# Attention with grouped keys: two early loads held back until the first has landed, and one set of transposes moved behind the third score chunk

## The chip, the cores and the metric

The kernel runs on one core of one Trainium2 chip. The metric is the device time of one execution in microseconds (us). PE is the matmul engine, ACT the engine that takes exponentials, DVE and POOL the two other vector engines, SP the engine whose queue issues most loads. A trace is one profiled execution; its span runs from the first to the last instruction and is about 1.7 us shorter than the device time. A load is issued by a queue and, some us later, lands: then all its data are there and the engines that wait for it may go on. PE starts at half clock and its granted clock then rises to full: in the trace of before the record of the clock has the rise at 4.57 us, the six weight loads of fillers from 3.8 to 4.3 us take 151 ns each, and those after 5.9 us 98 ns.

## The reference, cut to what matters

```python
B, Hq, Hkv, Sq, Sk, D = 16, 32, 8, 288, 512, 128      # bf16, four query heads per key head
scores = einsum("bhqd,bhkd->bhqk", q, k) * D ** -0.5
p = softmax(scores, axis=-1)
out = einsum("bhqk,bhkd->bhqd", p, v)
```

There are 16 x 8 = 128 groups. A group is the 4 x 288 = 1152 query rows that share one K and one V of 512 rows. The kernel cuts a group into three chunks, so there are 384 chunks.

## The kernel before

For chunk n PE computes the transposed scores S(n) = K Q^T (1536 columns of PSUM), ACT takes exp of all of them in one instruction, and two chunks later (`LAG`) PE multiplies by V: PV(n-2). DVE scales and stores. A column of ones beside V gives the row sums.

K and Q must have D on the partitions. Most come by transposed loads from SP. K of groups 0 and 1 take another way, to be there sooner: ACT's queue loads them plainly and PE transposes them. Q of group 0 comes in three transposed loads, one for each chunk.

```python
def op_kd(eng, g):                       # plain load of K of group g (0 or 1)
    eng.dma_start(kd_sb[:, g], kd_v[:, g]).then_inc(sem["s_kd%d" % g], 16)
def op_kt(g, tiles, bank): ...           # PE: four 128x128 transposes into ps_o
def op_kc(g, tiles, bank, n): ...        # DVE: copies them into kt_sb (s_k<g>)
def op_q0(i):                            # one third of Q of group 0
    c0, c1 = i * TPC, (i + 1) * TPC
    nc.sync.dma_start_transpose(qt_sb[:, 0, c0:c1], q_v[0:P, c0 * D:c1 * D]).then_inc(sem["s_qp%d" % i], 16)
def op_warm(n, w, dst): ...              # n filler matmuls on zeros, w columns each
# ... cut ...
first = [lambda i=i: op_q0(i) for i in range(NC)]           # SP: Q of group 0 in thirds,
first += [lambda: op_q(1), lambda: op_k(0, 2), lambda: op_q(2), lambda: op_v(0, None, 2, UG), lambda: op_q(3)]

@block.tensor
def _(eng):
    op_warm(WARM, BANK, ps_o[:, 1])
    op_kt(0, range(NJ), 0)
    op_warm(6, P, ps_s[:, 1])
    for n in range(NS):
        if n == LAG:
            op_kt(1, range(NJ), 1)
            op_warm(4, P, ps_o[:, 0])
        op_s(n)                          # waits: K, Q, and ACT's chunk n-2 (two PSUM halves)
        if n >= LAG:
            op_pv(n - LAG)

@block.scalar
def _(eng):
    op_kd(eng, 0)
    emit(eng, [("s_one", 1)], lambda: eng.activation(dum[:, 1:2], dum[:, 0:1], ACTF.Exp))
    op_v(0, eng, 0, 2)                   # V of groups 0 and 1
    op_kd(eng, 1)
    for n in range(NS):
        op_exp(n)
# ... cut: POOL copies V beside the ones, DVE scales, checks of the sums ...
```

Of the kernel before, what the change touches and what calls it, by code (L numbers as in the profile page):

```python
# [123 lines left out]
def bass_standalone__gqa_softmax__near_ridge_kernel(  # L124
# [5 lines left out]
):  # L130
    B, Hq, Sq, D = q.shape
    _, Hkv, Sk, _ = k.shape
    P = 128
    R = (Hq // Hkv) * Sq
    NJ = Sk // P
# [13 lines left out]
    LAG = 2  # L149
# [20 lines left out]
    with ExitStack() as es:  # L170
# [31 lines left out]
        def choose(eng, key):  # L202
            eng.wait_ge(sem["s_flag"], 1)
            reg = eng.alloc_register("bad_" + key)
            eng.load(reg, flag_i[:])
            if key == "sp":
                for (s, n) in need(eng, stored()):
                    eng.wait_ge(s, n)
            eng.br_ne(reg, 0, "general_" + key, "done_" + key)
            with nc.body("general_" + key):  # L210
                if key == "sp":
                    eng.sem_inc(sem["s_go"], 1)
                fns[key](eng)
                eng.br("done_" + key)
            nc.switch_bb("done_" + key)
# [18 lines left out]
        ps_s = main.enter_context(nc.psum_tensor("ps_s", [P, 2, CH], FP32))  # L234
# [4 lines left out]
        def need(eng, waits):  # L239

            left = []
            for (s, n) in waits:
                key = (id(eng), s)
                if seen.get(key, 0) < n:
                    seen[key] = n
                    left.append((sem[s], n))
            return left

        def emit(eng, waits, fn):
            waits = need(eng, waits)  # L250
            for (s, n) in waits[:-1]:
                eng.wait_ge(s, n)
            ins = fn()
            if waits:
                ins.wait_op(waits[-1][0], waits[-1][1], "sem-ge")
            return ins
# [3 lines left out]
        def op_kd(eng, g):  # L260
            eng.dma_start(kd_sb[:, g], kd_v[:, g]).then_inc(sem["s_kd%d" % g], 16)
# [12 lines left out]
        def op_v(u, eng=None, g0=0, g1=UG):  # L274
            eng = eng or nc.sync
            sl = u % NSLOT
            if u >= NSLOT:
                for (s, n) in need(eng, [("s_vc", UG * (u - NSLOT + 1))]):
                    eng.wait_ge(s, n)
            eng.dma_start(  # L280
                vd_sb[:, sl, g0:g1], v_v[:, u * UG + g0:u * UG + g1]
            ).then_inc(sem["us_v%d" % sl if u > 0 else "s_v%d" % g0], 16)
# [13 lines left out]
        def have_q(g, i):  # L296
            if g == 0:
                return ("s_qp%d" % i, 16)
            return ("s_q%d" % (g % NQ), 16 * (g // NQ + (0 if g % NQ == 0 else 1)))

        def have(kind, g):

            u = g // UG
            if u == 0 and kind == "k":
                return ("s_k%d" % min(g, 2), (1, 1, 16)[min(g, 2)])
            if u == 0:
                return ("s_v%d" % (g // 2 * 2), 16)
            return ("us_%s%d" % (kind, u % NSLOT), 16 * (u // NSLOT + (0 if u % NSLOT == 0 else 1)))
# [22 lines left out]
        def op_kt(g, tiles, bank):  # L331

            eng = nc.tensor
            dst = ps_o[:, bank].bitcast(BF16)
            for x, j in enumerate(tiles):
                ins = emit(eng, [("s_id", 2), ("s_kd%d" % g, 16)], lambda: eng.transpose(  # L336
                    dst[:, x * P:(x + 1) * P], kd_sb[:, g, j * D:(j + 1) * D], ident[:]))
            ins.then_inc(sem["s_kp"], 1)
# [7 lines left out]
        def op_warm(n, w, dst):  # L346

            for x in range(n):
                emit(nc.tensor, [("s_z", 1)], lambda: nc.tensor.matmul(  # L349
                    dst[:, 0:w], z_sb[:, 0:P], z_sb[:, 0:w], start=True, stop=True))  # L350

        def op_s(n):
            eng = nc.tensor
            g, i = n // NC, n % NC
            sl, gi = (g // UG) % NSLOT, g % UG
            waits = [have("k", g), have_q(g, i)]
            if n >= 2:
                waits.append(("s_e", n - 1))
            qg = qt_sb[:, g % NQ, i * TPC:(i + 1) * TPC].rearrange("d t p -> d (t p)")
            for x, (c, j, r0, w) in enumerate(pieces):  # L360
                ins = emit(eng, waits if x == 0 else [], lambda: eng.matmul(  # L361
                    ps_s[:, n % 2, c:c + w], kt_sb[:, sl, j, gi, :], qg[:, r0:r0 + w], start=True, stop=True))
                if n == 0 and c + w == BANK:
                    ins.then_inc(sem["s_s0"], 1)
            ins.then_inc(sem["s_s"], 1)
# [7 lines left out]
        def op_pv(r):  # L373
            eng = nc.tensor
            g = r // NC
            sl, gi = (g // UG) % NSLOT, g % UG
            waits = [("s_vc", g + 1), ("s_e", r + 1)]
            if 2 <= r < NS - 1:
                waits.append(("s_ev", r - 1))


            for j in range(NJ):
                for a in range(TPC):
                    ins = emit(eng, waits if a == 0 and j == 0 else [], lambda: eng.matmul(  # L384
                        outs(r)[:, a, :], pt_sb[:, r % NPT, j, a * P:(a + 1) * P],
                        v_sb[:, sl, gi * NJ + j, 0:DV], start=(j == 0 and a == 0), stop=(j == NJ - 1),
                        skip_group_check=True))
            ins.then_inc(sem["s_pv"], 1)

        def op_pv_last(a):  # L390

            eng = nc.tensor
            sl, gi = (LASTG // UG) % NSLOT, LASTG % UG
            for j in range(NJ):
                ins = emit(eng, [("s_e", NS + (0 if a < TPC - 1 else 1))], lambda: eng.matmul(  # L395
                    outs(NS - 1)[:, a, :], pt_sb[:, (NS - 1) % NPT, j, a * P:(a + 1) * P],
                    v_sb[:, sl, gi * NJ + j, 0:DV], start=(j == 0), stop=(j == NJ - 1)))
            if a == TPC - 1:
                ins.then_inc(sem["s_pv"], 1)


        def op_exp(n):
            eng = nc.scalar
            waits = [("s_s", n + 1)]
            if n >= NPT:
                waits.insert(0, ("s_pv", n - NPT + 1))
            dst, src = pt_sb[:, n % NPT], ps_s[:, n % 2].rearrange("p (j r) -> p j r", r=TW)
            parts = [(dst.rearrange("p j r -> p (j r)"), ps_s[:, n % 2])]
            if n == 0:
                d, s = parts[0]  # L410
                emit(eng, [("s_s0", 1)], lambda: eng.activation(d[:, 0:BANK], s[:, 0:BANK], ACTF.Exp, scale=scale))  # L411
                parts = [(d[:, BANK:CH], s[:, BANK:CH])]
            if n == NS - 1:
                w = TW - P
                parts = [(dst[:, :, 0:w], src[:, :, 0:w]), (dst[:, :, w:TW], src[:, :, w:TW])]
            for (d, s) in parts:
                emit(eng, waits, lambda: eng.activation(d, s, ACTF.Exp, scale=scale)).then_inc(sem["s_e"], 1)  # L417
# [84 lines left out]
        @block.sync  # L502
        def _(eng):
            for fn in first:
                fn()
            for (_, fn) in sp:
                fn()
            choose(eng, "sp")

        @block.tensor  # L510
        def _(eng):
            op_warm(WARM, BANK, ps_o[:, 1])
            op_kt(0, range(NJ), 0)
            op_warm(6, P, ps_s[:, 1])
            for n in range(NS):
                if n == LAG:
                    op_kt(1, range(NJ), 1)
                    op_warm(4, P, ps_o[:, 0])
                op_s(n)
                if n >= LAG:  # L520
                    op_pv(n - LAG)
            for r in range(NS - LAG, NS - 1):
                op_pv(r)
            for a in range(TPC):
                op_pv_last(a)
            emit(eng, [("s_ev", NS - 1), ("s_bad", 2)], lambda: eng.matmul(  # L526
                ps_o[0:1, NS % 2, 0:ALONE + 1], one_f[:], bad_sb[:, 1, :], start=True, stop=True)
            ).then_inc(sem["s_bad"], 1)
            choose(eng, "pe")

        @block.scalar
        def _(eng):
            op_kd(eng, 0)
            emit(eng, [("s_one", 1)], lambda: eng.activation(dum[:, 1:2], dum[:, 0:1], ACTF.Exp))  # L534
            op_v(0, eng, 0, 2)
            op_kd(eng, 1)
            for n in range(NS):
                op_exp(n)
            op_ev_act()
            choose(eng, "act")  # L540
# [72 lines left out]
```

## Time and profile before

| | |
|---|---|
| time, median (range) of the first 3 runs | 527.37 us (527.22 to 528.51) |
| span of the trace | 525.4 us |
| PE busy, ACT busy | 99%, 99% |
| ACT per chunk, end to end | 1.343 us |
| S(0) starts, first activation starts | 5.24, 5.67 us |
| S(2), S(3) start | 7.23, 8.78 us |

Two engines at 99% tell nothing about which one sets the pace; the prediction takes that from the starts and ends of single chunks. Three more lines of the timeline before are needed later: the first two score chunks, twelve matmuls, in 1.48 us; the first activation; and the weight loads of S(2), released by ACT.

```profile
5.24 1.48 PE L361 MATMUL ps_s<-qt_sb,kt_sb 128*128 128x384 bf16 x12 [0.52 <-DMA qt_sb<-in_q_dram]
5.67 0.60 ACT L411 ACTIVATE pt_sb<-ps_s 128x512 bf16<-128x512 f32 x1 [2.95 <-PE ps_s L361]
...
7.23 0.55 PEld L361 LDWEIGHTS ps_s<-qt_sb,kt_sb 128*128 128x128 bf16 x6 [0.24 <-ACT pt_sb L417]
```

Below, the start of S(0), S(2) or S(3) is that of its first weight load (PEld, the weight loads of PE); its first matmul follows within 0.11 us.

### The profile page before, as it was taken

How to read it: one execution, taken by the hardware profiler on the slowest of the kernel's cores; microseconds unless marked ns; L12 is line 12 of the kernel's file. 1: busy time of each engine (PE TensorE's matmuls, PEld its weight loads, DVE VectorE, ACT ScalarE, POOL GpSimd, SP SyncE). 2: the span in 40 equal slices, each digit the busy share in tenths (PEclk: the TensorE clock that was granted, in tenths of full speed). 3: DMA queues.
4: the chain of work that ended last, by engine and by line, in shares of the span. 5: the costliest groups of instructions: out<-in, count | busy, mean ns of one | idle time of the engine just before them, and what ended most of it. 6: DMA issues, size and time to landing. Idle time of an engine off the chain costs nothing.

```text
span 525.4 us, 16369 instructions
## 1 busy us (share of the span) xinstructions
PE 520.5 (99%) x6937; PEld 456.7 (87%) x6937; DVE 289.7 (55%) x812; ACT 517.9 (99%) x389; POOL 74.3 (14%) x135
## 2 busy tenths in 40 slices
PE   8999999999999999999999999999999999999997
PEld 6888888888888888888888888888888888888886
DVE  2555555555555555555555555555555555555555
ACT  6999999999999999999999999999999999999997
POOL 1210111111111101111111011110111101111000
PEclk9999999999999999999999999999999999999999
DMA  8999999899999999999999999999999999887112
GB/s 158 216 226 247 229 242 250 227 197 238 240 221 237 245 209 205 211 231 229 223 232 208 232 180 255 242 212 193 224 218 237 209 208 190 236 204 195 69 70 91
DMA packets 253143, 110.12 MB, mean 210 GB/s; under 512 B 219792, under 2 KB 236816, under 8 KB 253072
## 3 DMA queue, kind: packets, MB, share of 16 engines
q1 hardware_dynamic: 252512, 108.56, 97.3%
q8 instruction: 55, 0.90, 0.7%
q10 hardware_dynamic: 560, 0.52, 0.4%
q14 instruction: 16, 0.13, 0.1%
HBM read 17.04 MB, written 37.75 MB: 104 GB/s over the span
## 4 chain that ended last, share of the span: by engine, by line
PE 98%; DMA 1%; ACT 0%; DVE 0%; issue 0%
PE ps_o L384 50%; PE ps_s L361 48%; DMA qt_sb<-in_q_dram 1%; ACT pt_sb L417 0%; PE ps_s L395 0%; ACT pt_sb L411 0%; DVE o_sb L454 0%; PE ps_o L526 0%; DVE bad_sb L480 0%; DVE rl_sb L434 0%; DVE flag_i L580 0%; DVE bad_sb L477 0%
## 5 line engine op out<-in xcount | busy, mean ns | idle before, releaser
L417 ACT ACTIVATE pt_sb<-ps_s 128x1536 bf16<-128x1536 f32 (+1 forms) x385 | 515.6, 1746 | 0.0
L384 PE MATMUL ps_o<-v_sb,pt_sb 128*128 128x129 bf16 x4596 | 322.9, 220 | 0.0
L361 PE MATMUL ps_s<-qt_sb,kt_sb 128*128 128x384 bf16 (+2 forms) x2304 | 317.1, 274 | 0.7 <-DMA qt_sb<-in_q_dram 0.5
L384 PEld LDWEIGHTS ps_o<-v_sb,pt_sb 128*128 128x128 bf16 x4596 | 291.9, 98 | 24.8
L444 DVE TENSOR_TENSOR o_sb<-ps_o,rl_sb 128x384 bf16<-128x384 f32 x383 | 213.5, 558 | 13.3
L361 PEld LDWEIGHTS ps_s<-qt_sb,kt_sb 128*128 128x128 bf16 x2304 | 178.9, 98 | 37.5 <-DMA qt_sb<-in_q_dram 0.8
L434 DVE RECIPROCAL rl_sb<-ps_o 128x3 f32<-128x3 f32 x383 | 69.3, 181 | 213.9 <-PE ps_o L384 213.9
L427 POOL COPY v_sb<-vd_sb 128x512 bf16<-128x512 bf16 x128 | 73.3, 616 | 408.3 <-DMA vd_sb<-in_v_dram 383.7
L349 PE MATMUL ps_o<-z_sb 128*128 128x512 bf16 (+1 forms) x9 | 2.7, 447 | 1.3 <-DVE z_sb L555 1.3
L343 DVE COPY kt_sb<-ps_o 128x512 bf16<-128x512 bf16 x2 | 0.8, 425 | 5.3 <-PE ps_o L336 5.3
L411 ACT ACTIVATE pt_sb<-ps_s 128x512 bf16<-128x512 f32 x1 | 0.6, 598 | 2.9 <-PE ps_s L361 2.9
L470 DVE TENSOR_REDUCE st_sb<-rl_sb 128x1 f32<-128x72 f32 (+1 forms) x16 | 3.5, 216 | 0.0
L472 DVE TENSOR_REDUCE st_sb<-rl_sb 128x1 f32<-128x72 f32 (+1 forms) x16 | 3.5, 216 | 0.0
L349 PEld LDWEIGHTS ps_o<-z_sb 128*128 128x128 bf16 x9 | 0.9, 119 | 2.1 <-DVE z_sb L555 1.3
L534 ACT ACT_TABLE_LOAD x1 | 1.3, 1283 | 1.2 <-PEq L598 1.2
L336 PEld LDWEIGHTS ps_o<-ident,kd_sb 128*128 128x128 bf16 x8 | 0.7, 114 | 0.9 <-DMA kd_sb<-in_k_dram 0.8
L526 PE MATMUL ps_o<-bad_sb,one_f 128*1 128x25 f32 x2 | 0.2, 184 | 1.0 <-DVE bad_sb L480 1.0
L526 PEld LDWEIGHTS ps_o<-bad_sb,one_f 128*1 128x1 f32 x2 | 0.1, 80 | 1.2 <-DVE bad_sb L480 1.2
L461 ACT ACTIVATE o_sb<-ps_s,rl_sb 128x128 bf16<-128x128 f32 x1 | 0.4, 367 | 0.7 <-DVE rl_sb L434 0.7
L336 PE MATMUL ps_o<-ident,kd_sb 128*128 128x128 bf16 x8 | 1.0, 263 | 0.0
L395 PE MATMUL ps_s<-v_sb,pt_sb 128*128 128x129 bf16 x12 | 0.9, 222 | 0.0
L395 PEld LDWEIGHTS ps_s<-v_sb,pt_sb 128*128 128x128 bf16 x12 | 0.7, 98 | 0.2 <-ACT pt_sb L417 0.2
(22 smaller groups left out, 5.1 us busy)
## 6 DMA issues: line engine op xcount, KB each, us to landing
out_dram<-o_sb SPq DMA_DIRECT2D x127, 288.0 KB, 4.1
vd_sb<-in_v_dram SPq DMA_DIRECT2D x31, 512.0 KB, 5.5
qt_sb<-in_q_dram SPq DMA_TRANSPOSE x130, 5.0
kt_sb<-in_k_dram SPq DMA_TRANSPOSE x32, 5.3
out_dram<-o_sb SPq DMA_DIRECT2D x3, 96.0 KB, 1.6
kd_sb<-in_k_dram ACTq DMA_DIRECT2D x2, 128.0 KB, 3.2
vd_sb<-in_v_dram ACTq DMA_DIRECT2D x1, 256.0 KB, 3.7
vd_sb<-in_v_dram SPq DMA_DIRECT2D x1, 256.0 KB, 4.9
```

The lines of the kernel that those rows point to most:

```text
L336: ins = emit(eng, [("s_id", 2), ("s_kd%d" % g, 16)], lambda: eng.transpose(dst[:, x * P:(x + 1) * P], kd_sb[:, g, j * D:(j + 1) * D], iden ...
L349: emit(nc.tensor, [("s_z", 1)], lambda: nc.tensor.matmul(dst[:, 0:w], z_sb[:, 0:P], z_sb[:, 0:w], start=True, stop=True))
L361: ins = emit(eng, waits if x == 0 else [], lambda: eng.matmul(ps_s[:, n % 2, c:c + w], kt_sb[:, sl, j, gi, :], qg[:, r0:r0 + w], start=Tru ...
L384: ins = emit(eng, waits if a == 0 and j == 0 else [], lambda: eng.matmul(outs(r)[:, a, :], pt_sb[:, r % NPT, j, a * P:(a + 1) * P], v_sb[: ...
L395: ins = emit(eng, [("s_e", NS + (0 if a < TPC - 1 else 1))], lambda: eng.matmul(outs(NS - 1)[:, a, :], pt_sb[:, (NS - 1) % NPT, j, a * P:( ...
L417: emit(eng, waits, lambda: eng.activation(d, s, ACTF.Exp, scale=scale)).then_inc(sem["s_e"], 1)
L427: emit(eng, waits, lambda: eng.tensor_copy(v_sb[:, sl, gi * NJ:(gi + 1) * NJ, 0:D], vd_sb[:, sl, gi].rearrange("p (j d) -> p j d", d=D))). ...
L434: emit(eng, [("s_pv", r + 1)], lambda: eng.reciprocal(rl_sb[:, TPC * r:TPC * (r + 1)].unsqueeze(2), outs(r)[:, :, D:DV])).then_inc(sem["s_ ...
L444: emit(eng, waits, lambda: eng.tensor_tensor(out=o_sb[:, g % NO, t0:t0 + TPC, :], in0=outs(r)[:, :, 0:D], in1=rl_sb[:, TPC * r:TPC * (r + ...
L470: emit(eng, [("s_rc", e // TPC)], lambda: eng.tensor_reduce(st_sb[:, 0, b:b + 1], rl_sb[:, a:e], AX.X, ALU.max))
L472: eng.tensor_reduce(st_sb[:, 1, b:b + 1], rl_sb[:, a:e], AX.X, ALU.min).then_inc(sem["s_stat"], 1)
L534: emit(eng, [("s_one", 1)], lambda: eng.activation(dum[:, 1:2], dum[:, 0:1], ACTF.Exp))
```

## The change

The intent: K of group 0 and the first third of Q are what the first scores need. V of groups 0 and 1 and K of group 1 were issued beside them and took the DMA engines. They now wait until K of group 0 has landed, K of group 1 first. As K of group 1 comes later, its transposes move behind S(2), and two more fillers bridge the time before S(0).

```diff
 def _(eng):                      # PE
     op_warm(WARM, BANK, ps_o[:, 1])
     op_kt(0, range(NJ), 0)
-    op_warm(6, P, ps_s[:, 1])
+    op_warm(8, P, ps_s[:, 1])
     for n in range(NS):
-        if n == LAG:
-            op_kt(1, range(NJ), 1)
+        if n == 2:
             op_warm(4, P, ps_o[:, 0])
         op_s(n)
+        if n == 2:
+            op_kt(1, range(NJ), 1)
         if n >= LAG:
             op_pv(n - LAG)
@@                                # ACT
     op_kd(eng, 0)
     emit(eng, [("s_one", 1)], lambda: eng.activation(dum[:, 1:2], dum[:, 0:1], ACTF.Exp))
+    for (s, n) in need(eng, [("s_kd0", 16)]):
+        eng.wait_ge(s, n)
+    op_kd(eng, 1)
     op_v(0, eng, 0, 2)
-    op_kd(eng, 1)
```

## The prediction

> **What bounds the kernel now.** I first read the page: busy shares, then the costliest groups.
>
> ```profile
> PE 520.5 (99%) x6937; PEld 456.7 (87%) x6937; DVE 289.7 (55%) x812; ACT 517.9 (99%) x389; POOL 74.3 (14%) x135
> ...
> L417 ACT ACTIVATE pt_sb<-ps_s 128x1536 bf16<-128x1536 f32 (+1 forms) x385 | 515.6, 1746 | 0.0
> ```
>
> PE and ACT are both at 99%, so busy shares cannot say which one sets the pace. The work is 384 chunks (128 groups of three): PE makes scores S(n), ACT takes the exponential, PE multiplies by V two chunks later (PV(n-2)). I therefore read the timeline of ACT alone, in two windows that start early and end at different places, and of PE, early and late.
>
> ```profile
> 6.16 2.36 ACT L417 ACTIVATE pt_sb<-ps_s 128x1024 bf16<-128x1024 f32 x2
> ...
> 7.07 134.45 ACT L417 ACTIVATE pt_sb<-ps_s 128x1536 bf16<-128x1536 f32 x100
> ```
>
> Chunk 1 ends at 6.16 + 2.36 = 8.52 us, chunk 100 at 7.07 + 134.45 = 141.52. That is 133.00 / 99 = 1.3434 us per chunk. PE's score chunks start at 10.14, 11.48 and 12.81 early (1.335 apart) and at 141.57 and 142.92 late (1.343 apart): left alone PE needs 1.335, later it follows ACT. **ACT is the bound, by 0.0085 us per chunk, from its first activation on.** Check: the first activation starts at 5.67; 384 x 1.3434 = 515.9; the span is 525.4, which leaves 3.8 us for the last PV, its scaling and the flag. The diff touches none of that. So it can act only through (a) the time at which ACT starts and (b) whether ACT is starved in the first chunks. Both are decided before 10 us. Now that stretch, first the timeline:
>
> ```profile
> 0.82 0.38 ACTq L261 DMA_DIRECT2D kd_sb<-in_k_dram  x1
> ...
> 0.82 3.90 SPq L294 DMA_TRANSPOSE qt_sb<-in_q_dram  x3
> ...
> 1.29 0.39 ACTq L280 DMA_DIRECT2D vd_sb<-in_v_dram  x1
> ...
> 1.71 0.54 ACTq L261 DMA_DIRECT2D kd_sb<-in_k_dram  x1
> ...
> 3.90 0.83 PE L349 MATMUL ps_s<-z_sb 128*128 128x128 bf16 x6
> 4.14 0.42 DVE L343 COPY kt_sb<-ps_o 128x512 bf16<-128x512 bf16 x1 [2.91 <-PE ps_o L336]
> 4.77 1.35 SPq L289 DMA_TRANSPOSE qt_sb<-in_q_dram  x1
> 5.01 1.17 POOL L427 COPY v_sb<-vd_sb 128x512 bf16<-128x512 bf16 x2 [3.37 <-DMA vd_sb<-in_v_dram]
> 5.24 1.21 PEld L361 LDWEIGHTS ps_s<-qt_sb,kt_sb 128*128 128x128 bf16 x12 [0.76 <-DMA qt_sb<-in_q_dram]
> ```
>
> S(0) starts at 5.24, released by the first third of Q, issued at 0.82 and 4.4 us in flight by the view of its line (landing 5.2). K of group 0 was transposed and copied by 4.56, so Q is last, by 0.6 us. Why Q is late shows in the DMA view of 3.25 to 4.5 us, by queue (q1 is SP's, q10 ACT's):
>
> ```profile
> q10 hardware_dynamic: 344, 0.33, 103.5%
> q1 hardware_dynamic: 81, 0.01, 6.3%
> ```
>
> V of groups 0 and 1 and K of group 1 take all 16 engines while the end of Q's first third stands behind them.
>
> **What the Trainium skill says.** "DMA: Bandwidth & Descriptors", section "Issuing engines are not separate DMA queues": loads started from ACT and SP run on the same 16 DMA engines and interleave. The trace agrees (103.5% against 6.3%). "TensorE: Matmul & The Clock Gate", Part 1: the array runs at half clock until it has been busy some 3.4 us, in a window that is free-running. The trace agrees: five 512-column matmuls take 2.32 us early, while from 5.24 on six score matmuls (1536 columns) pass in 0.66. "ScalarE: Activation LUTs", What ACT_TABLE_LOAD costs: 186 ns + 0.833 ns per element, overlapping the next by 93; for 1536 that is 1466 and 1373. The trace has 1457 to 1470 for an unhindered one, but 1343 from end to end, so I use the trace.
>
> **The change part by part.**
>
> *K of group 1 and V are held until K of group 0 has landed.* That landing is 3.45 (issue 0.82 plus 2.6). The first third of Q then meets no big loads: its data are read by about 3.3, and I estimate its landing at 4.1 to 4.4 instead of 5.2. S(0) is then released by the next latest of two: the copy of K at 4.56, and PE itself.
>
> *Filler matmuls 6 -> 8.* At half clock they are 0.107 us apart (0.43 per 512 columns, divided by 4), so PE is free at 3.90 + 8 x 0.107 = 4.75. I put S(0) at 4.7 and the first activation 0.43 later (as 5.24 -> 5.67), at 5.15: **ACT starts 0.5 us sooner.** If nothing followed, the kernel would be 0.5 us faster.
>
> *Transposes of K of group 1 after S(2).* Four matmuls of 0.056 us, 0.22 in all. Before, they lay in PE's wait for bank 0 (0.24 us of idle even so); now they lie between S(2) and PV(0), when both have work. S(2) waits for ACT's chunk 0 (start 7.23 before, 6.7 after), ends its issue 0.67 later, transposes to 7.6, PV(0) takes 12 x 0.057 = 0.68 to 8.3. S(3) also needs DVE's copy of these transposes: start 0.26 after the last one's, 0.42 long, some 0.1 to reach PE: 8.2 to 8.3. No loss against the 8.8 below.
>
> *What S(3) waits for.* S(3) is the first chunk of group 1. Before, it started so:
>
> ```profile
> 7.74 0.83 PEld L384 LDWEIGHTS ps_o<-v_sb,pt_sb 128*128 128x128 bf16 x12
> 8.78 0.46 PEld L361 LDWEIGHTS ps_s<-qt_sb,kt_sb 128*128 128x128 bf16 x5 [0.21 <-ACT pt_sb L417]
> ```
>
> The view blames ACT, but chunk 1 of ACT had ended at 8.52, and PV(0) had been issued by 8.58. In the code S(3) also waits for Q of group 1. Its transposed load is issued at 4.77, 3.9 us to landing in the view of its line: 8.67, and 0.1 later S(3) starts. So **Q of group 1 is the wait that ends last there, and SP issues it at a fixed 4.77 behind the three thirds (1.3 us each)**; the diff does not move it. Its slack before: S(3) ends at 8.81 + 0.82 = 9.63, ACT could start on it at 9.67; ACT ran chunk 2 from 8.40 to 9.87, and as one activation overlaps the next by 1.46 - 1.34 = 0.12, chunk 3 was due at 9.75. Slack 0.09 us.
>
> *Sum.* Start 0.5 sooner; but S(3) stays at 8.78 or later, so chunk 3 of ACT can begin at 9.67 instead of 9.75: ACT stands still for about 0.4 us, and **0.09 of the 0.5 us is left**. Against that, V is now issued near 3.45 + 0.05 + 0.45 = 3.95 and flows around 5.5 to 6.8, where the load of Q of group 1 starts (the DMA view has no packet at all from 5.75 to 6.15, then q1 at 96%). 256 KB at the 276 GB/s of the 3.25 to 4.5 stretch is 0.9 us of the engines; I guess that 0.1 to 0.4 of it falls on Q of group 1. Net: -0.09 + 0.2 = about +0.1 us.
>
> **The rivals.** *1. The whole half microsecond is kept (526.9).* For it: Q's first third is the only wait at 5.2, and the change removes what holds it. Against it: the landing at 8.67. It needs that load to speed up by 0.4 us, and from 5.7 to 8.7 it already had the engines with nothing from ACT's queue. *2. V becomes the bound (527.6 to 528.1).* V took 3.7 us from issue; from 3.95 that is 7.6. POOL's copy (1.17 for two, 0.6 for one) and two hops make PV(0) start at 8.35 and S(3) at 9.0, 0.25 later than before; with 4.9 us to landing, as SP's V load had, 1.4 later. For it: the times just quoted. Against: in the kernel before V met Q's descriptors and shared its start with two loads; alone it should be nearer 3.3. *3. The clock comes late.* If the granted clock rose after S(0), the first chunks would be slower by up to 0.6 us each, in both kernels alike. *4. All is hidden (527.3).* That is my sum with no harm to Q of group 1.
>
> **Range and chances.** The three timed runs of before lie 1.3 us apart, more than any effect here. Middle: 527.37 + 0.1 = 527.5. Down: rival 1 and noise, 526.8. Up: rival 2 and noise, 528.3. Two per cent is 10.5 us; no rival gets there, the whole start before the first activation is 5.7. Chances: faster 0.005, same 0.985, slower 0.01.
>
> **What would show it right or wrong.** First activation at 5.0 to 5.25 (before 5.67); if it is still at 5.6, ACT's loads were not what held Q. S(3) at 8.75 to 9.1: if it is near 8.4, Q of group 1 landed earlier and rival 1 holds; if PV(0) starts after 8.2 and S(3) follows it without a gap, rival 2 holds. ACT should show a standstill of 0.3 to 0.6 us before its chunk 3, and then the same 1.343 per chunk. The prediction is wrong if the steady pace changes, or if a later group waits for a load that has fallen behind.

## The result, and the profile after

The changed kernel took 527.25 us (median of 4 runs, 527.00 to 527.68); the kernel before, on the same chip and beside it, 527.30 (527.12 to 528.51). The ratio is 0.9995, interval 0.9978 to 1.0012: the same. (A ratio is the mean of one kernel's fast runs over that of the other's in the same rounds, so not quite the ratio of the medians.)

The trace, however, is not the same. The page of the changed kernel, its busy shares and ACT's group:

```profile
PE 521.3 (99%) x6939; PEld 457.2 (87%) x6939; DVE 289.8 (55%) x812; ACT 518.4 (99%) x389; POOL 74.1 (14%) x135
...
L417 ACT ACTIVATE pt_sb<-ps_s 128x1536 bf16<-128x1536 f32 (+1 forms) x385 | 515.9, 1738 | 0.5 <-PE ps_s L361 0.3
```

ACT now has an idle entry (0.5 us, released by the score matmuls); before it had 0.0. The span is 526.0, 0.6 longer than the trace before. The timeline of the changed kernel shows where (columns: start, duration, engine, line, operation, operands, count, idle time before and what ended it):

```profile
3.01 0.34 ACTq L261 DMA_DIRECT2D kd_sb<-in_k_dram  x1
...
3.38 0.46 ACTq L280 DMA_DIRECT2D vd_sb<-in_v_dram  x1
...
4.66 2.56 PE L361 MATMUL ps_s<-qt_sb,kt_sb 128*128 128x384 bf16 x12
...
5.33 0.60 ACT L411 ACTIVATE pt_sb<-ps_s 128x512 bf16<-128x512 f32 x1 [2.59 <-PE ps_s L361]
...
6.18 4.03 ACT L417 ACTIVATE pt_sb<-ps_s 128x1024 bf16<-128x1024 f32 x3 [0.26 <-PE ps_s L361]
...
7.91 0.81 PE L361 MATMUL ps_s<-qt_sb,kt_sb 128*128 128x384 bf16 x6 [0.46 <-DMA qt_sb<-in_q_dram]
...
8.98 0.42 DVE L343 COPY kt_sb<-ps_o 128x512 bf16<-128x512 bf16 x1 [4.51 <-PE ps_o L336]
9.48 0.56 PEld L361 LDWEIGHTS ps_s<-qt_sb,kt_sb 128*128 128x128 bf16 x6
...
10.36 2.79 ACT L417 ACTIVATE pt_sb<-ps_s 128x1536 bf16<-128x1536 f32 x2
```

Read it from the top. K of group 1 and V are issued at 3.01 and 3.38. S(0) starts its weight load at 4.59, and the first activation begins at 5.33 instead of 5.67: the intended gain, 0.34 us. Then it goes. The twelve matmuls of S(0) and S(1) take 2.56 us against 1.48: the clock is still at half. S(2) starts at 7.88 (its matmuls at 7.91), and a load of Q released it, where ACT did before at 7.23. (The view puts the weight load at 7.88 down to ACT, but ACT's chunk 0 had ended at 7.21.) S(3) starts at 9.48 instead of 8.78.

Which Q is it that S(2) waits for? The last third of group 0, issued at 3.49. The view of that line gives 4.3 us to landing (7.77 in the trace; 6.09 before):

```profile
L294 SPq DMA_TRANSPOSE qt_sb<-in_q_dram x1: 1260/1260/1260, 3.5 to 3.5; - x1
...
DMA to landing us min/median/max: 4.3/4.3/4.3
```

The DMA view of the changed kernel from 4.75 to 5.55 us, just ahead of that third's data, by queue (packets, MB, share of 16 engines):

```profile
q10 hardware_dynamic: 163, 0.17, 67.8%
q1 hardware_dynamic: 2, 0.00, 0.1%
```

This is the picture that the kernel before had at 3.25 to 4.5 us, moved by 1.5 us: ACT's queue has the engines, SP's queue stands. Before, it stood in front of the first third of Q; now it stands in front of the last. That is not the whole delay, though. Q of group 0 is the first 288 KB on SP's queue; counted in the packets of the traces, the last of them had gone by 5.58 us before and by 6.29 in the changed kernel, 0.71 later, while the landing came 1.7 later. The rest lies between the last packet and the landing: 0.51 us before, 1.48 now. That lag is 1.35 and 1.40 us in two later traces with the old order too (e5, e3), where the last third landed at 7.28 and 7.20. What sets it was not tested. From chunk 3 on nothing else is different. The timeline of ACT alone has

```profile
10.36 131.75 ACT L417 ACTIVATE pt_sb<-ps_s 128x1536 bf16<-128x1536 f32 x98
```

so chunk 100 ends at 142.11, chunk 4 at 10.36 + 2.79 = 13.15, and (142.11 - 13.15) / 96 = 1.343 us per chunk, as before.

**An account that closes.** Before, chunk 4 of ACT ended 6.885 us after the first activation started (12.555 - 5.670). What a trace takes over 6.885 there is called "still" below: time that ACT lost. Changed kernel: 13.152 - 5.330 - 6.885 = 0.94. So 0.34 was won, 0.94 lost, net 0.60, which is the difference of the spans. Of the 0.94, 0.5 is the idle time that the page shows; most of the other 0.4 is overlap that went with it: back to back an activation starts 0.10 to 0.15 us before the last one ends, and after each of the four breaks it did not. This account is used for every trace below.

So one trace shows a loss and the timing shows none. Either the trace of the changed kernel is a slow one (its run took 527.68, the slowest of its four) or the trace of before is a fast one. The experiments had to settle that too.

### The profile page after: what moved, and what is told of

Read it like the earlier page. It is cut to its first block, busy times and chain, and to the rows that moved or that the text cites. A ratio compares the mean times of both kernels' runs of the same rounds, so it can differ in the third digit from the quotient of the medians.

```text
span 526.0 us, 16373 instructions
## 1 busy us (share of the span) xinstructions
PE 521.3 (99%) x6939; PEld 457.2 (87%) x6939; DVE 289.8 (55%) x812; ACT 518.4 (99%) x389; POOL 74.1 (14%) x135
## 4 chain that ended last, share of the span: by engine, by line
PE 98%; DMA 1%; SPq 0%; DVE 0%; issue 0%
PE ps_o L384 50%; PE ps_s L361 48%; DMA qt_sb<-in_q_dram 1%; SPq L294 0%; PE ps_s L395 0%; DVE o_sb L454 0%; PE ps_o L527 0%; PE ps_o L336 0%; DVE bad_sb L480 0%; DVE rl_sb L434 0%; DVE flag_i L583 0%; DVE bad_sb L477 0%
## 5 line engine op out<-in xcount | busy, mean ns | idle before, releaser
L349 PE MATMUL ps_s<-z_sb 128*128 128x128 bf16 x8 | 1.1, 314 | 0.0
```

The costliest lines, as they stand in the source:

```text
L349: emit(nc.tensor, [("s_z", 1)], lambda: nc.tensor.matmul(dst[:, 0:w], z_sb[:, 0:P], z_sb[:, 0:w], start=True, stop=True))
```

## The experiments

Every run that is listed gave a correct result. First the times. "Slow" counts runs of 528.3 us or more; the times of before leave a gap there (nothing between 527.97 and 528.36), though of the variants 528.01, 528.19 and 528.35 lie in it. The calls ran on different chips, so times are compared inside a call. The diffs below are shortened: waits and semaphores that go with an edit are left out.

| run | median (range), us | slow | ratio (interval) | before: median, slow |
|---|---|---|---|---|
| changed kernel, first result | 527.25 (527.00-527.68) | 0 of 4 | 0.9995 (0.9978-1.0012) | 527.30, 1 of 4 |
| e1 changed kernel again | 527.40 (527.14-527.70) | 0 of 6 | 0.9987 (0.9974-1.0000) | 527.70, 5 of 11 |
| e2 order of loads only | 527.42 (527.22-528.41) | 1 of 6 | 0.9993 (0.9979-1.0007) | same |
| e3 PE's part only | 527.37 (527.33-527.98) | 0 of 6 | 0.9989 (0.9975-1.0002) | same |
| e4 changed, half of V | 527.55 (527.09-528.46) | 1 of 6 | 0.9992 (0.9978-1.0007) | same |
| e5 before again | 527.89 (527.22-528.89) | 2 of 6 | 0.9990 (0.9974-1.0007) | 528.58, 7 of 11 |
| e6 changed + merged Q | 527.24 (527.08-527.29) | 0 of 5 | 0.9980 (0.9964-0.9997) | same |
| e7 before + merged Q | 528.88 (527.20-529.16) | 4 of 6 | 1.0007 (0.9989-1.0025) | same |
| e8 before, one look | 528.36 | 1 of 1 | - | same |
| e9 before, 12 fillers | 527.47 (527.20-528.63) | 1 of 6 | 0.9997 (0.9983-1.0010) | 527.95, 5 of 11 |
| e10 changed, 0 fillers | 527.18 (527.05-527.97) | 0 of 5 | 0.9988 (0.9975-1.0001) | same |
| e11 changed + merged, V first | 527.33 (527.23-527.64) | 0 of 5 | 0.9988 (0.9976-1.0001) | same |
| e12 changed + merged, half of V | 527.76 (527.71-528.49) | 2 of 5 | 1.0002 (0.9989-1.0015) | same |

Then the traces, one for each, in us. "Clock" is when the granted clock of PE rises to full in the record of the trace; "still" is the account above. The first six load in the old order.

| trace | clock | last third of Q lands | S(2) | Q of group 1 lands | S(3) | first activation | still | span |
|---|---|---|---|---|---|---|---|---|
| before | 4.57 | 6.09 | 7.23 | 8.67 | 8.78 | 5.67 | 0.00 | 525.35 |
| e8 before | 8.88 | 6.24 | 8.68 | 9.09 | 10.12 | 6.04 | 0.90 | 526.62 |
| e5 before | 9.62 | 7.28 | 8.99 | 9.23 | 10.64 | 6.36 | 1.11 | 527.14 |
| e3 PE's part only | 7.36 | 7.20 | 8.16 | 9.15 | 9.75 | 6.23 | 0.36 | 526.28 |
| e7 before + merged Q | 4.34 | 6.31 | 7.42 | 7.53 | 8.75 | 5.80 | 0.02 | 525.50 |
| e9 before, 12 fillers | 4.22 | 6.15 | 7.30 | 8.96 | 9.07 | 5.74 | 0.12 | 525.55 |
| changed | 6.88 | 7.77 | 7.88 | 9.20 | 9.48 | 5.33 | 0.94 | 525.95 |
| e1 changed | 5.40 | 7.51 | 7.62 | 9.43 | 9.53 | 5.33 | 0.99 | 526.00 |
| e2 order of loads only | 4.46 | 7.72 | 7.83 | 8.89 | 9.14 | 5.04 | 0.92 | 525.64 |
| e10 changed, 0 fillers | 4.50 | 7.42 | 7.52 | 8.73 | 9.12 | 5.04 | 0.88 | 525.60 |
| e4 changed, half of V | 5.94 | 6.31 | 7.22 | 9.35 | 9.45 | 5.33 | 0.91 | 526.32 |
| e6 changed + merged Q | 4.25 | 5.81 | 6.69 | 8.68 | 8.99 | 5.04 | 0.77 | 525.49 |
| e11 same, V first | 5.95 | 6.50 | 7.38 | 7.74 | 9.01 | 5.33 | 0.67 | 525.69 |
| e12 same, half of V | 6.29 | 5.27 | 7.26 | 8.44 | 9.52 | 5.33 | 1.01 | 526.02 |

The account closes: against the trace of before, the later first activation plus "still" gives the longer span, to 0.01 us (e8: 0.37 + 0.90 = 1.27; 526.62 - 525.35 = 1.27; e5: 0.69 + 1.11 = 1.80 and 1.79). e4 alone has 0.39 more, later on. As "still" is taken from the end of chunk 4, what this shows is that nothing after chunk 4 differs.

**e1: the changed kernel again** (no edit).

> The changed kernel once more, for a second trace. In the first one the last third of Q landed at 7.77 us (6.09 before the change) and S(2) started at 7.88 (7.23 before); the granted clock rose only at 6.9 us (4.6 in the trace of before). Theory V: V, issued at 3.4, takes the DMA engines just ahead of the last third of Q, so S(2) is late whatever the clock does: again 7.6 to 8.0, and S(3) at 9.2 to 9.6. Rival clock: the late clock cost the time; if it rises before 5.5 here, S(2) starts below 7.3 and S(3) below 9.0. Time against before: 0.999 to 1.001 by either.

Measured: the clock rose at 5.40, before the rival's 5.5, and still S(2) started at 7.62 and S(3) at 9.53. PE's timeline in this run:

```profile
4.66 1.84 PE L361 MATMUL ps_s<-qt_sb,kt_sb 128*128 128x384 bf16 x12
...
7.65 0.81 PE L361 MATMUL ps_s<-qt_sb,kt_sb 128*128 128x384 bf16 x6 [0.92 <-DMA qt_sb<-in_q_dram]
...
9.56 0.81 PE L361 MATMUL ps_s<-qt_sb,kt_sb 128*128 128x384 bf16 x6 [0.20 <-DMA qt_sb<-in_q_dram]
```

With less half clock (1.84 us for the twelve) PE merely waits longer, 0.92 us, for the same load. So a late clock is not needed for the loss: with the clock up at 5.40 "still" is 0.99, and at 4.5 in e2 and e10 it is 0.92 and 0.88.

**e2: the order of the loads only.**

```diff
 # changed kernel, PE as before:
-    op_warm(8, P, ps_s[:, 1])
+    op_warm(6, P, ps_s[:, 1])
-        if n == 2: op_warm(4, ...)        # op_kt(1) back ahead of op_s(2)
+        if n == LAG: op_kt(1, range(NJ), 1); op_warm(4, ...)
```

> The changed order of the loads, with PE's order and 6 fillers as before (transposes of K of group 1 ahead of S(2)). Theory V: S(2) still waits for the last third of Q until 7.6 to 8.0; the transposes then lie in that wait, so S(3) starts about 0.15 to 0.22 us sooner than in the changed kernel, at 9.2 to 9.35, where Q of group 1 (landing 9.2) holds it. Rival place: putting the transposes behind S(2) is what loses the gain; then S(3) would come back to 8.8 and the time would be 0.4 us or more under before. Theory V: time within 0.3 us of before.

Measured: S(2) at 7.83, S(3) at 9.14. PE's timeline in this run:

```profile
6.09 0.39 PE L336 MATMUL ps_o<-ident,kd_sb 128*128 128x128 bf16 x4
...
7.86 0.81 PE L361 MATMUL ps_s<-qt_sb,kt_sb 128*128 128x384 bf16 x6 [1.16 <-DMA qt_sb<-in_q_dram]
8.51 0.84 PE L384 MATMUL ps_o<-v_sb,pt_sb 128*128 128x129 bf16 x12
9.19 0.82 PE L361 MATMUL ps_s<-qt_sb,kt_sb 128*128 128x384 bf16 x6
```

The transposes ran at 6.09, in the wait, and S(3) followed PV(0) with no gap. The place of the transposes is thus worth a little, 0.3 us in the start of S(3), but S(2) is as late as ever, and with it ACT's standstill (0.92). The place is not what loses the gain.

**e3: PE's part only** (the changed kernel with ACT's loads as before).

```diff
-    for (s, n) in need(eng, [("s_kd0", 16)]): eng.wait_ge(s, n)
-    op_kd(eng, 1)
     op_v(0, eng, 0, 2)
+    op_kd(eng, 1)
```

> PE's new order (8 fillers, transposes behind S(2)) with the loads ordered as before. Theory V: S(0) 5.2, S(2) 7.2, both as before; PV(0) shifts by 0.22 and ends its issue at 8.81, so S(3) starts at 8.8 to 9.0 against 8.78; ACT had 0.09 us of slack there, so the time is 0 to 0.15 us over before. Rival place: S(3) at 9.4 or later as in the changed kernel, 0.6 us over before.

The starts missed the expectation: S(0) 5.59, S(2) 8.16, S(3) 9.75, each 0.4 to 1.0 us late. That read as the rival until the other columns were seen: the first third of Q landed at 5.55 (5.20 before) and the clock rose at 7.36. S(2) was released by ACT, not by Q, and "still" is 0.36, which is what the half clock cost between the first activation and the second (0.37 in e8 and in the changed kernel too). So PE's part costs nothing in this trace; the start was late for another reason, and that reason had to be looked for in the kernel before (e5, e8). None of the six runs is slow, where before had five of eleven; that comes up again below.

**e4: half of V.** V of group 1 is issued when ACT's first chunk is done.

```diff
-    op_v(0, eng, 0, 2)
+    op_v(0, eng, 0, 1)
     for n in range(NS):
         op_exp(n)
+        if n == 1: wait s_e >= 1; op_v(0, eng, 1, 2)
```

> The changed kernel, but only V of group 0 is loaded behind K of group 1; V of group 1 (half of the bytes) is issued when the first chunk of ACT is done, about 7.2 us. Theory V: the last third of Q has half as much ahead of it and lands 0.3 to 0.6 us sooner, 7.2 to 7.5, S(2) starts at 7.25 to 7.55, S(3) 0.2 to 0.4 us sooner than in the changed kernel; time 0.2 to 0.4 us under it. Rival clock or place: S(2) and S(3) where the changed kernel has them, same time. V of group 1 must land by 11.4 us or PV(3) waits.

Measured: the last third of Q landed at 6.31 instead of 7.77, better than expected, and S(2) started at 7.22, released by ACT. PE's timeline in this run:

```profile
7.22 0.83 PE L361 MATMUL ps_s<-qt_sb,kt_sb 128*128 128x384 bf16 x6 [0.24 <-ACT pt_sb L417]
...
9.48 0.81 PE L361 MATMUL ps_s<-qt_sb,kt_sb 128*128 128x384 bf16 x6 [0.53 <-DMA qt_sb<-in_q_dram]
```

So V's bytes held the last third of Q: one trace against four of the new order with all of V, where it landed at 7.42 to 7.77. The packets of Q of group 0 had gone by 5.86 (6.29 in the changed kernel), and the lag to the landing was 0.45 us. It did not bring the time back: S(3) now waits for Q of group 1, which landed at 9.35, and "still" is 0.91. The expected gain at S(3) was a miss. There was a second price. V of group 1 moved into the later loads, Q of group 5 landed at 25.86, and its first chunk, due at about 25.45 behind the work on PE, started at 25.97: 0.39 us more.

**e5 and e8: the kernel before, again** (no edit).

> The kernel before, unchanged, against itself: what the timing alone scatters, and a second trace of it. Of the 15 timed runs so far 6 took 528.4 us or more and the others about 527.4; the one trace is of a fast one (527.04). Ratio 1.000 within 0.0015. Theory start: ACT never waits for scores after its first activation whatever the clock does, and a slow run is one in which the first activation or the clock came late. Rival: a slow run lost its time later, at a group whose load fell behind, or the steady pace itself differs from 1.3434 us.

> One more trace of the kernel before, for the scatter of the clock (4.6 us in its first trace, 4.5 to 7.4 in the five others) and of the landings of Q (first third 5.2, group 1 8.7). Theory start: time = first activation + what the clock takes + 384 x 1.3434 + 3.8.

Both traces are of slow runs (528.89 and 528.36). The expectation that ACT never waits after its first activation was wrong: it stood still for 1.11 and 0.90 us. PE's timeline of e8:

```profile
5.39 2.74 PE L361 MATMUL ps_s<-qt_sb,kt_sb 128*128 128x384 bf16 x12 [0.63 <-DMA qt_sb<-in_q_dram]
7.93 0.63 PE L336 MATMUL ps_o<-ident,kd_sb 128*128 128x128 bf16 x4
8.36 0.63 PE L349 MATMUL ps_o<-z_sb 128*128 128x128 bf16 x4
8.78 0.87 PE L361 MATMUL ps_s<-qt_sb,kt_sb 128*128 128x384 bf16 x6
```

Twelve matmuls in 2.74 us and four transposes in 0.63 (0.39 at full clock): PE was at half clock until 8.88. A mean weight load took 151 ns in this stretch, 98 in the fast trace. S(2) starts at 8.7 with no wait for a load; PE is simply late. So in both slow traces of before the clock rises late, and the first activation is late too (6.04 and 6.36). The first trace of before, 525.35, was the best of all fourteen. Four of its five companions in the old order are longer by 0.15 to 1.3 us, one by 1.8.

**e6 and e7: the last two thirds of Q in one load**, in the changed kernel and in the kernel before.

```diff
-    c0, c1 = i * TPC, (i + 1) * TPC
+    c0, c1 = (0, TPC) if i == 0 else (TPC, NT)      # op_q0(0), op_q0(1)
```

> The changed kernel, with the second and third third of Q's first group loaded by one transfer. A transfer of nine tiles takes SP about as long to issue as one of three (1.36 and 1.25 to 1.31 us), so Q of group 1 is issued at 3.5 instead of 4.8, and the last third of Q goes ahead of V. Theory V: the last two thirds land by 5.4 to 6.0, S(2) waits for ACT alone, at 6.6 to 7.2; Q of group 1 lands at 7.6 to 8.3; S(3) starts at 8.2 to 8.7 (V and the copy of K of group 1 next in line) instead of 9.5; ACT loses 0.4 us or less after its first activation, clock aside, and the time is 0.4 to 0.8 us under the changed kernel. Rival: if the DMA engines, not the order, are the limit, the landings stay at 7.5 and 9.2, and so does the time.

> The kernel before with the same merged transfer. In its trace ACT did not wait after its first activation, so there is nothing to win behind it: S(3) can start at 8.6 instead of 8.78, S(0) stays at 5.2 to 5.6 and the time within 0.3 us of before. If it is 0.4 us or more faster, Q of group 1 did cost time in most runs of before and the one trace was a lucky one.

e6: Q's two thirds landed at 5.81 and S(2) waited for no load, as expected; S(1), which now needs the same load, started at 5.85 and cost 0.28 of standstill. S(3) came at 8.99, later than expected: V landed at 7.64, POOL's copy ended at 8.30, and PV(0) started at 8.36; V had become the wait (the prediction's second rival). "Still" is 0.77, 0.17 less than in the changed kernel. The trace is 0.46 shorter; the other 0.29 is the first activation, sooner by an early clock. The five times lie within 0.21 us, and the ratio to before is 0.9980: no other kernel has its whole interval below 1. That comes from the seven slow runs of before in this call: its four others have a median of 527.19. Against the changed kernel e6 was not measured; its median, 527.24, is no better than 527.25, so the 0.4 to 0.8 us that were expected are not seen.

e7: Q of group 1 landed at 7.53 and S(3) had 1.1 us to spare, yet nothing came of it: first activation 5.80, "still" 0.02, span 525.50, and four slow runs in six. In the old order the wait for Q of group 1 costs little when the clock is early (e9, with Q of group 1 landing at 8.96, lost 0.12 to it).

**e9 and e10: fillers added to before, and taken from the changed kernel.**

```diff
-    op_warm(6, P, ps_s[:, 1])    # e9, kernel before
+    op_warm(12, P, ps_s[:, 1])
-    op_warm(8, P, ps_s[:, 1])    # e10, changed kernel
+    op_warm(0, P, ps_s[:, 1])
```

> The kernel before with 12 filler matmuls instead of 6, nothing else. Two slow traces of before (528.36 and 528.89 us) have the clock rise at 8.9 and 9.6 us; no trace with 8 fillers or the new order of loads has it later than 7.4. Theory clock: PE stands idle from 4.7 us until Q lands (5.2 to 5.7), and a clock window with that hole in it does not count as busy[...]. 12 fillers end at about 5.2 and close the hole: no run of 528.2 us or more in six, trace with the clock by 7.7, median 0.3 us or more under that of before where that has slow runs in the same call. Rival: slow runs come from the loads; then 12 fillers change nothing: slow runs as often as in before.

> The changed kernel with no fillers after the first transposes (0 instead of 8). S(0) still waits for the copy of K, at 4.6, as in the changed kernel, so the loads and the chain of waits stay the same; only PE idles from about 3.8 to 4.6. Theory clock: slow runs come back, two or more of six 0.8 us or more above the fastest, with the clock rising after 8 us in such a trace. Rival: it is the order of the loads that removed the slow runs; then all six lie within 0.7 us, as the changed kernel's.

e9: one slow run of six (528.63) and one of 528.19, where before had five of eleven: fewer, but the expectation was none. e10: no slow run of five, though one is 0.92 us above the fastest, where the rival allowed 0.7; the trace has S(0) at 4.59 and the clock at 4.50. So the fillers are not what keeps slow runs away in the changed kernel. My theory of the fillers is not borne out. It may be the order of the loads, by which PE has real work from 4.6 us on: over all runs listed, 4 of 42 with the new order are slow and 26 of 62 with the old. But this is not shown: e3, with the old order and PE's new part, had no slow run of six, and e2, with the new order and PE as before, had one of six, of which there is no trace.

**e11 and e12: merged Q with V ahead of K of group 1, and with half of V.** Edits as in e6, with the two lines of ACT's loads swapped (e11) or as in e4 (e12).

> The changed kernel with the merged transfer of Q's last two thirds (S(3) then started at 8.99, held by V: landing 7.64, copy until 8.30, PV(0) 8.36), and V ahead of K of group 1. Theory: V lands 0.4 to 0.9 us sooner, 6.7 to 7.2, PV(0) starts at 7.5 to 8.0, S(3) at 8.5 to 8.8, where Q of group 1 or the copy of K of group 1 hold it; 0.2 to 0.4 us under the merged one. Rival: V ahead of Q's last two thirds delays those (5.8), S(1) and S(2) wait, and the gain is lost there: same time.

> The merged transfer, and V of group 1 held until ACT's first chunk is done (half of V's bytes out of the way). Theory: V of group 0 lands at 6.2 to 6.8, PV(0) can start at 7.6, Q of group 1 lands 0.2 to 0.6 us sooner than 8.68; S(3) at 8.2 to 8.6 against 8.99, 0.3 to 0.6 us under the merged one unless a later Q (group 5 in the earlier run with half of V) falls behind and takes it back. Rival: landings are set by SP's queue alone; S(3) stays near 8.8.

e11: V landed at 6.05, sooner than expected, but the two thirds of Q at 6.50 instead of 5.81. S(1) waited for them until 6.54, which is half of the standstill of 0.67 (the other half is half clock). S(3) started at 9.01, when the copy of the transposed K had ended at 8.94. The rival was right: a load moved up was paid by the next. e12 missed: with half of its bytes V landed at 8.17, later than the whole V in e6 (7.64), and S(3) came at 9.52. Why a smaller load came later is not explained.

## Why the prediction was right or wrong

The time, 527.25 against 527.5 predicted, and "the same" were right. That says little for the mechanism: the range was 1.5 us wide because the runs of before scatter by more than the effect, and a gain and a loss that were both mis-sized end near zero. The steps were right in part.

- **ACT is the bound and only the first 10 us count**: right. The pace after chunk 3 is 1.343 us in the changed kernel, and start plus standstill gives the span of every trace but e4's.
- **ACT starts 0.5 us sooner, at 5.15**: the mechanism was right, the size off. The first third of Q landed at 3.49 (I said 4.1 to 4.4), S(0) started at 4.59 (4.7). But the first activation needs 0.43 us after S(0) only at full clock (5.04 in e2 and e10); at half clock it was 0.74, so 5.33. The term mis-sized is "0.43 later".
- **"S(2) waits for ACT's chunk 0 (start 7.23 before, 6.7 after)": this step failed.** S(2) waited for the last third of Q, which landed at 7.77, and started at 7.88. I let V fall on Q of group 1; but V flowed at 4.8 to 6, earlier than my 5.5 to 6.8, and what it met was the last third, still on its way. One cause of that is a landing that I took from the trace of before: K of group 0 at 3.45. It too was freed of the loads beside it and landed at 2.99, so V was issued at 3.38 and not at 3.95. e4 supports the reading: half of V, landing 6.31 instead of 7.77. That the packets went later accounts for 0.71 us of the 1.7 by which the landing moved; the longer lag behind the last packet stays unexplained.
- **S(3) held by Q of group 1 at 8.8**: half right. That load was the last to arrive in e1 (9.43, S(3) at 9.53) and in e4. In the changed kernel's first trace it landed at 9.20, but PV(0) was issued, and the copy of the transposed K ended, only by 9.41, after which S(3) started at 9.48. "No loss against the 8.8" for the transposes failed with the step before: S(2) was late, so the transposes behind it were late as well (e2: S(3) 0.34 sooner with them ahead of it).
- **0.09 of the 0.5 us is left, then +0.1 net**: the sign of the small sum held in the trace, the size not (+0.6; ACT lost 0.94 and not 0.4). (By its own figures, 9.75 and 9.67, the slack is 0.08.) I took 8.67 as the landing of Q of group 1; in the five traces with the old order and three thirds it is 8.67 to 9.23, and I had the lowest.
- **Rival 3, a late clock "in both kernels alike": not as far as these runs go.** Of 44 timed runs of before 21 are slow; of 10 of the changed kernel none is. Before was slow most often in a call in which the changed kernel did not run; in the two calls with both, it is 6 of 15 against 0 of 10. Both slow traces have the clock at 8.9 and 9.6; none of the eight traces with the new order has it after 6.9. The two ratios put the mean 0.05 and 0.13% lower (0.3 and 0.7 us), with intervals that reach 1. Among runs that are not slow the kernels hardly differ: in e1's call the six of before have a median of 527.48, the six of the changed kernel 527.40.

So the expected gain at the start was real (first activation at 5.04 to 5.33 in eight traces of the new order, at 5.67 to 6.36 in six of the old). It was given back at S(2) and S(3): by the wait for the last third of Q, which V's new place lengthened, and by the waits that stood behind it. What may remain shows in the times as fewer slow runs. What stays open: which part of the change does that, the loads or PE's part (e3); and whether it makes a late clock rarer or makes it cost less, because PE would wait for Q until 7.5 to 7.9 anyway. No trace of the new order with a clock later than 6.9 exists, and three of its variants (e2, e4, e12) had slow runs too.

## What to carry to other kernels

A landing that is read from the old trace moves when the loads beside it move: do not carry it over as fixed. A load that is pushed back does not vanish; find the next small load behind it on the same DMA engines and check that chunk's slack, not only the first one's. When the change is under a microsecond, one trace of each kernel is not a comparison: take several, and read landings and the rise of the clock in each before sizing a slack from them. Write the first stretch as an account (first start plus standstill) that must add up to the span; where it does not, as in e4, something later has changed.

## What the Trainium skill lacked or had wrong

- "TensorE: Matmul & The Clock Gate", Part 1, puts the rise around 4 us into sustained activity, give or take 0.5 us, and says elsewhere on the page that it varies by run. Here PE worked from 1.27 us in every kernel, and the rise came at 4.2 to 9.6 us, so 3.0 to 8.4 later. In the two traces above 8 us PE had idled 0.63 and 0.74 us just ahead of S(0); in e7 it idled 0.81 there, but the clock was up before, at 4.34. The page does not say how large a hole makes a window not count; e9 and e10 did not settle it.
- "DMA: Bandwidth & Descriptors", section "Issuing engines are not separate DMA queues", has the loads of all queues share 16 engines and interleave. Both traces agree on the sharing, but show little interleaving in these stretches: one queue moved while the other nearly stood (103.5% against 6.3% before, 67.8% against 0.1% after). It gives no feeling for the size: the first third of Q landed 2.7 us after its issue in the changed kernel and 4.4 before, with V and K of group 1 beside it.
- The same page, "DMA Transpose (X-bar)", gives no issue time, and the page has none for loads of three or nine tiles. A transposed load took SP 1.23 to 1.31 us to issue for three tiles and 1.36 for nine in the trace of before; the same nine took 1.92 in the changed kernel, and later loads of nine 1.32 to 2.99 (before, up to 40 us). So three times the tiles did not take three times as long.
- No page tells how far landings scatter between runs of one kernel: Q of group 1, 3.9 to 4.5 us from issue in five traces with the same order.
